# Two attention layers and two gated layers: norms of the gated layers on ScalarE, q's phi over ScalarE and VectorE, scans fetched from ScalarE, output units between q units

## Chip, cores, metric

One core of a Trainium2 chip. The metric is the device time of one execution in microseconds; before, the median of 3 runs is 1562.31 us (1561.06 to 1563.51). Engines go by the profile's names: PE (TensorE's matmuls), PEld (its weight loads), DVE (VectorE), ACT (ScalarE), POOL (GpSimd) and SP (SyncE, which issues DMAs).

## The reference, cut

S = 2048 rows (16 tiles of 128), D = 1024, F = 3584, 32 heads of 32. Four layers in turn, A B A B, with the same weights for both A and both B:

```python
def _A_ref(x, wqkv, wo):
    q, k, v = ...                      # x @ wqkv, by heads
    phi = lambda t: jnp.where(t > 0, t + 1, jnp.exp(t)) + 1e-6
    pq, pk = phi(q), phi(k)
    kv = jnp.einsum("bhsd,bhse->bhde", pk, v)
    z = jnp.einsum("bhsd->bhd", pk)
    num = jnp.einsum("bhqd,bhde->bhqe", pq, kv)
    den = jnp.einsum("bhqd,bhd->bhq", pq, z)[..., None] + 1e-6
    return (num / den) ... @ wo

def _B_ref(x, w_gate, w_up, w_down):
    h = (x @ w_gate) * (x @ w_up)
    return h @ w_down

x = x + _A_ref(_layernorm(x), A_wqkv, A_wo)
x = x + _B_ref(_layernorm(x), B_w_gate, B_w_up, B_w_down)
...                                    # the same two again
```

## The kernel before, in words

Nothing is scheduled by a compiler: the order in which the Python code emits instructions is the order on each engine, and every engine works strictly through its own row of instructions. An instruction that waits holds up all that stands behind it on its engine, DMA issues on SP too. x stays in SBUF (`X`, bf16). The eight large tiles `K[0]` to `K[7]`, and `W`, `TX`, `ST`, `MX`, are used again and again for different things; eight PSUM banks `Q[0]` to `Q[7]` are handed out in turn by `mm_tile`, so a matmul group can start when the group eight places before it has been read out of its bank.

**Layer A** (`layer_A`) runs in units, each a group of matmuls into one bank and what reads it out. k units (`k_unit`) give pk; 16 xk units give X^T pk (16 matmuls, a copy on ACT, L327); 32 q units (`q_unit`, two for a tile of rows) do 8 matmuls and `phi`: an exponential on ACT (L295), a minimum on DVE (L296) and, again from the bank, a maximum on DVE (L297). After a tile's second q unit `over_den` (L366) multiplies and sums on DVE, and SP transposes the tile by DMA (`tx`, L274). `kv_unit` and 16 kvo units (`kvo_unit`, one matmul each, copied by ACT at L394 into `KVo`) put kv and wo together. 32 output units (`out_unit`) do 8 matmuls each, and DVE adds the bank to X (`add_x`, L397).

In the first layer A, **scans** run beside this: gate, up and down weights are loaded in 42 pieces of 512 KB, and ACT squares and sums each (`scan_step`, L213) for a scale of each matrix (`scale_sum`, `scale_pow`, into `fac` and `kap`). Pieces share a few buffers, and a piece is fetched when its buffer's last piece has been scanned (`scan_fetch`, L198), by SP.

**The turn to a gated layer.** The last q units and the first output units alternate in a loop of nine (L672). Beside the output units the norm of the next layer is made for the first 8 tiles: `norm_fill` with DVE's statistics (L245, L249), POOL's power (L251 to L270) and ACT's application (`ln_apply_act`, L272) into `ST`, which holds four tiles, so the second four wait for the transposes of the first. `t_fill` (L466) forms sums of transposed tiles on DVE. `prep` converts a unit's weights on ACT (L435) and forms four sums (L438), here on POOL.

**Layer B** (`layer_B`) computes gate and up with a seven-product scheme on 2 x 2 blocks: for a unit u of 14, `gate_step(u, p)` does product p (8 matmuls into two banks) and reads it out. Product 1 needs only transposed tiles; 5, 6 and 4 need the first, second and fourth `t_fill` sum, 7 the third. The down weights get the same kind of sums in the first B layer (`down_prep`: fetch, scale on ACT, four sums on DVE, store to DRAM), spread over the units.

The order around the change, in the words of the code: `spread(main, fill)` emits a unit of main and then its share of fill. The two lines that set the turn are

```python
        spread(o[18:26], fill[9] + norm_fill(1, 1, xn_b, True))
        spread(o[26:], t_fill() + prep(1, nc.gpsimd) + (list(down_prep(0)) if first_A else []))
```

## Time and profile before

| | us |
|---|---|
| median of 3 runs | 1562.31 |
| the profiled execution | 1563.76 |
| its span | 1562.0 |
| PE busy | 1489.7 (95%) |
| DVE busy | 1114.4 (71%) |
| ACT busy | 691.9 (44%) |
| mean granted clock of TensorE | 0.986 |

Span is from the first instruction to the last; the execution's own time is a little longer. A row of the timeline gives start, duration, engine, line, operation, output and inputs, a count of merged instructions and, in brackets, the idle time before it and what ended it. A row of the groups gives busy time and mean ns of one, then the idle time before them.

### The profile page before, as it was taken

How to read it: one execution, taken by the hardware profiler on the slowest of the kernel's cores; microseconds unless marked ns; L12 is line 12 of the kernel's file. 1: busy time of each engine (PE TensorE's matmuls, PEld its weight loads, DVE VectorE, ACT ScalarE, POOL GpSimd, SP SyncE). 2: the span in 40 equal slices, each digit the busy share in tenths (PEclk: the TensorE clock that was granted, in tenths of full speed). 3: DMA queues.
4: the chain of work that ended last, by engine and by line, in shares of the span. 5: the costliest groups of instructions: out<-in, count | busy, mean ns of one | idle time of the engine just before them, and what ended most of it. 6: DMA issues, size and time to landing. Idle time of an engine off the chain costs nothing.

```text
span 1562.0 us, 18309 instructions
## 1 busy us (share of the span) xinstructions
PE 1489.7 (95%) x6893; PEld 678.7 (43%) x6995; DVE 1114.4 (71%) x1834; ACT 691.9 (44%) x834; POOL 121.8 (8%) x194
## 2 busy tenths in 40 slices
PE   9899798599999999999999998979999999999999
PEld 3344343244444444444444444434444444444444
DVE  7766697688878467776668778977777755777633
ACT  4976653478750066661013224136665004666300
POOL 3500022200001000000110000340000000000000
PEclk9999999799999999999999999989999999999999
DMA  7957725377656523324752014162233573332342
GB/s 223 201 176 207 226 59 112 112 213 220 192 182 210 134 81 89 101 76 167 200 145 67 15 29 114 27 115 82 81 82 101 171 227 101 95 94 81 128 173 84
DMA packets 277049, 202.79 MB, mean 130 GB/s; under 512 B 102112, under 2 KB 264160, under 8 KB 273376
## 3 DMA queue, kind: packets, MB, share of 16 engines
q1 hardware_dynamic: 276960, 201.62, 46.0%
q8 instruction: 54, 0.88, 0.2%
q14 instruction: 35, 0.29, 0.1%
HBM read 160.43 MB, written 17.04 MB: 114 GB/s over the span
## 4 chain that ended last, share of the span: by engine, by line
PE 84%; DVE 7%; DMA 3%; ACT 3%; issue 2%; SPq 1%; POOL 0%; ACTq 0%; DVEq 0%
PE Q L473 43%; PE Q L725 22%; PE Q L307 9%; PE Q L325 7%; PE Q L405 3%; DMA XT<-ST 1%; DVE X L397 1%; DVE W L296 1%; DVE TX L438 1%; DVE st L245 1%; SPq L133 1%; ACT K L213 1%; ACT W L295 1%; DVE MX L369 1%; DVE K L297 1%
## 5 line engine op out<-in xcount | busy, mean ns | idle before, releaser
L473 PEld LDWEIGHTS <-K 128*128 128x128 f16 x3136 | 307.7, 98 | 409.8 <-issue 39.6
L473 PE MATMUL Q<-XT,K 128*128 128x512 bf16 (+1 forms) x1732 | 398.8, 382 | 35.1 <-DVE X L397 28.6
L725 PE MATMUL Q<-K,K 128*128 128x512 f16 (+1 forms) x1596 | 340.8, 375 | 1.0 <-DVE X L732 1.0
L473 PE MATMUL Q<-TX,K 128*128 128x512 f16 x1344 | 308.5, 379 | 3.8 <-ACT MX L495 2.1
L435 ACT ACTIVATE K<-K,fac 128x2048 f16<-128x2048 bf16 x112 | 218.3, 2000 | 128.2 <-DMA K<-in_B_w_gate_dram 127.4
L725 PEld LDWEIGHTS <-K 128*128 128x128 f16 x1596 | 155.1, 98 | 185.1 <-issue 1.3
L438 DVE TENSOR_TENSOR K<-K 128x1024 f16<-128x1024 f16 (+1 forms) x228 | 146.9, 665 | 35.5 <-ACT K L435 33.5
L295 ACT ACTIVATE W<-Q 128x512 bf16<-128x512 f32 x128 | 76.2, 599 | 211.0 <-PE Q L307 198.1
L438 DVE TENSOR_TENSOR W<-MX,Q 128x512 f16<-128x512 f32 x176 | 116.6, 684 | 32.0 <-ACT MX L495 18.0
L307 PE MATMUL Q<-K,K 128*128 128x512 bf16 x498 | 117.5, 387 | 5.7 <-DVE W L296 4.9
L438 DVE TENSOR_TENSOR W<-W,Q 128x512 f16<-128x512 f32 x160 | 105.6, 684 | 18.1 <-ACT W L495 11.5
L307 PE MATMUL Q<-K,XT 128*128 128x512 bf16 x500 | 113.6, 379 | 2.0 <-DMA XT<-ST 0.8
L495 ACT COPY MX<-Q 128x512 f32<-128x512 f32 x120 | 69.3, 585 | 100.3 <-PE Q L473 100.3
L296 DVE TENSOR_SCALAR W<-W 128x512 bf16<-128x512 bf16 x128 | 46.7, 365 | 72.0 <-ACT W L295 72.0
L495 ACT COPY W<-Q 128x512 f32<-128x512 f32 x104 | 60.4, 585 | 76.8 <-PE Q L473 76.2
L438 DVE TENSOR_TENSOR K<-K,K 128x512 f16<-128x512 f16 (+1 forms) x148 | 87.7, 597 | 4.2
L438 DVE TENSOR_TENSOR K<-W,Q 128x512 f16<-128x512 f16 x56 | 38.4, 687 | 72.6 <-PE Q L473 72.6
L245 DVE BATCH_NORM_STATS2 st<-X 128x6 f32<-128x512 bf16 x128 | 80.9, 673 | 3.5 <-DMA X<-in_A_x_dram 3.5
L307 PEld LDWEIGHTS <-K 128*128 128x128 bf16 x512 | 50.6, 100 | 67.6 <-DMA K<-ST 5.4
L251 POOL TENSOR_SCALAR ve<-mv 128x1 f32<-128x1 f32 x64 | 15.5, 242 | 819.7 <-DVE mv L249 819.7
L732 DVE SCALAR_TENSOR_TENSOR W<-Q,kap,X 128x512 f32<-128x512 f32 x32 | 24.0, 750 | 77.6 <-PE Q L725 77.6
L307 PEld LDWEIGHTS <-XT 128*128 128x128 bf16 x512 | 49.6, 98 | 61.7 <-ACT XT L290 1.4
(90 smaller groups left out, 1294.0 us busy)
## 6 DMA issues: line engine op xcount, KB each, us to landing
K<-WD SPq DMA_DIRECT2D x28, 1792.0 KB, 7.4
K<-in_B_w_gate_dram SPq DMA_DIRECT2D x70, 512.0 KB, 4.2
K<-in_B_w_up_dram SPq DMA_DIRECT2D x67, 512.0 KB, 4.9
K<-in_A_wqkv_dram SPq DMA_DIRECT2D x10, 1024.0 KB, 7.8
K<-in_B_w_down_dram SPq DMA_DIRECT2D x19, 512.0 KB, 5.2
WD<-K SPq DMA_DIRECT2D x10, 512.0 KB, 2.9
X<-in_A_x_dram SPq DMA_DIRECT2D x16, 256.0 KB, 5.3
out_dram<-X SPq DMA_DIRECT2D x31, 128.0 KB, 1.7
```

The costliest lines, as they stand in the source:

```text
L245: nc.vector.bn_stats(out=stat[t][0][:, c, :], in_=X[:, t, c * NB:(c + 1) * NB])
L295: nc.scalar.activation(out=e, in_=ps, func=ACT.Exp)
L296: nc.vector.tensor_scalar(out=e, in0=e, scalar1=1.0, scalar2=1e-6, op0=ALU.min, op1=ALU.add)
L307: nc.tensor.matmul(out=ps, lhsT=xt[:, k, tl * P:(tl + 1) * P], rhs=w[:, k, :], start=(k == 0), stop=(k == KD - 1))
L325: nc.tensor.matmul(out=ps, lhsT=xn_a[t][:, j * P:(j + 1) * P], rhs=pk[t][:, n * NB:(n + 1) * NB], start=(t == 0), stop=(t == NT - 1))
L405: nc.tensor.matmul(out=ps, lhsT=xT[t // TPG][:, c, tl * P:(tl + 1) * P], rhs=KVo[n][:, c, :], start=(c == 0), stop=(c == KD - 1))
L435: nc.scalar.activation(out=b.bitcast(F16), in_=b, func=ACT.Copy, scale=fac[:, m:m + 1])
L438: eng.tensor_tensor(out=o, in0=a, in1=b, op=op)
L473: nc.tensor.matmul(out=pair[m], lhsT=stationary(n, p, m, k), rhs=moving[p][:, k, :], start=(p in (1, 2, 5) and k == 0), stop=(k == KH - 1) ...
L495: nc.scalar.copy(out=snaps[u, p][:, m, :], in_=a[m])
L725: nc.tensor.matmul(out=ps_[:, lo:hi], lhsT=act[:, u, j * P:(j + 1) * P], rhs=w[:, u, lo:hi], start=(p in (1, 2, 5) and u == 0), stop=(u == ...
L732: stt(out=o, in0=ps_, scalar=kap[:, 0:1], in1=x, op0=ALU.mult, op1=ALU.add)
```

## The change

- `ln_act` and `norm_act` are new: the norms of a gated layer's first 8 tiles, three ACT passes each (a sum for the mean, a square with a sum for the variance, the application), with POOL's small operations between them. The second four tiles go to buffers of their own (`xn_c`, in K[0] to K[3]).
- `phi` can be split: ACT writes x + 1 + 1e-6 to SBUF as a second pass over the bank, and DVE takes the maximum in SBUF. It is used for q tiles 13 to 15 of the first A layer and for all q tiles of the second.
- The scans: more of them in the four-piece buffers (`EARLY` 30, `MID` 39), three for each of the first six q tiles, fetched by ACT from piece 14 on.
- The kvo units stand one q unit later, five or six after each of q units 20 to 22.
- `prep(0)` has its sums on DVE; `prep(1)` and the scan-dependent `down_prep` move: units 0 and 1 of `down_prep` (scale on DVE) into the first A layer, `prep(1)` into the gated layer's unit 0, and later fetches one unit earlier.
- The norm's pieces stand between the output units from the fifth round of the loop on, and `t_fill` behind the last four output units.

In the built program the eight banks Q[0] to Q[7] are called Q_83 to Q_90, K[0] to K[7] are K_74 to K_81, and XT_69 and XT_70 hold the transposed tiles of the first and second four.

On ACT, at the first turn, the rows behind the last q unit stood like this (the exponential of q unit 31, eight applications, the conversion of unit 1, the first `down_prep`, then the copies of product 1):

```order
L295 ACTIVATE W<-Q_84 128x512
L272 ACTIVATE ST<-X,off,rstd 128x1024 x8
L435 ACTIVATE K_80<-K_80,fac 128x2048 x2
L532 ACTIVATE K_74<-K_74,fac 128x2048
L491 COPY MX<-Q_83 128x512
L491 COPY MX<-Q_84 128x512
```

and the last rows ahead of product 1's copies are now (L285 a pass with the sum for the mean, L289 with the sum of squares, L295 the application; eight like them stand between these and q unit 31):

```order
L285 ACTIVATE K_76,sm<-X 128x1024
L289 ACTIVATE K_75,ss<-X,nm 128x1024
L295 ACTIVATE K_74<-X,of,rs 128x1024
L285 ACTIVATE K_77,sm<-X 128x1024
L289 ACTIVATE K_76,ss<-X,nm 128x1024
L295 ACTIVATE K_75<-X,of,rs 128x1024
L289 ACTIVATE K_77,ss<-X,nm 128x1024
L295 ACTIVATE K_76<-X,of,rs 128x1024
L295 ACTIVATE K_77<-X,of,rs 128x1024
L519 COPY MX<-Q_83 128x512
L519 COPY MX<-Q_84 128x512
L463 ACTIVATE K_80<-K_80,fac 128x2048 x2
```

The conversion of unit 1 (K_80) moved from ahead of product 1's copies to behind them, and the applications now have their own sums ahead of them, on the same engine.

On DVE, in the same place, the last bank sums (X<-X,Q) and the four `t_fill` sums (the rows with XT) stood like this:

```order
L438 TENSOR_TENSOR TX<-XT_70,XT_69 128x2048
L397 TENSOR_TENSOR X<-X,Q_88 128x512
L438 TENSOR_TENSOR TX<-XT_70,TX 128x2048
L438 TENSOR_TENSOR XT_70<-XT_70 128x2048
L397 TENSOR_TENSOR X<-X,Q_89 128x512
L438 TENSOR_TENSOR TX<-XT_69,TX 128x2048
L397 TENSOR_TENSOR X<-X,Q_90 128x512
L397 TENSOR_TENSOR X<-X,Q_83 128x512
L397 TENSOR_TENSOR X<-X,Q_84 128x512
```

and now:

```order
L425 TENSOR_TENSOR X<-X,Q_88 128x512
L425 TENSOR_TENSOR X<-X,Q_89 128x512
L466 TENSOR_TENSOR TX<-XT_70,XT_69 128x2048
L425 TENSOR_TENSOR X<-X,Q_90 128x512
L466 TENSOR_TENSOR TX<-XT_70,TX 128x2048
L425 TENSOR_TENSOR X<-X,Q_83 128x512
L466 TENSOR_TENSOR XT_70<-XT_70 128x2048
L425 TENSOR_TENSOR X<-X,Q_84 128x512
L466 TENSOR_TENSOR TX<-XT_69,TX 128x2048
```

Two and three `t_fill` sums stand ahead of the sums that free Q_83 and Q_84, where all four did.

On ACT in the first kvo stretch, the scans (the rows with acc) and what stands between them, from q unit 17 on, were

```order
L295 ACTIVATE W<-Q_84 128x512
L213 ACTIVATE K_74,acc<-K_74 128x2048
L295 ACTIVATE W<-Q_85 128x512
L213 ACTIVATE W,acc<-W 128x2048
L295 ACTIVATE W<-Q_86 128x512
L394 CAST K_77<-Q_87 128x512
```

and are now (the DMA rows are fetches of later pieces):

```order
L326 ACTIVATE W<-Q_84 128x512
L326 ACTIVATE W<-Q_85 128x512
L217 ACTIVATE W,acc<-W 128x2048
L209 DMA W<-in_B_w_down_dram 128x2x1024
L209 DMA K_74<-in_B_w_down_dram 128x2x1024
L209 DMA K_78<-in_B_w_down_dram 128x2x1024
L326 ACTIVATE W<-Q_86 128x512
L326 ACTIVATE W<-Q_87 128x512
L422 CAST K_77<-Q_88 128x512
```

Three of the scans moved to the q tiles ahead of this stretch, and the fetches moved from SP's row into ACT's.

The diff, cut to its core:

```diff
+    pb = [W[:, 6 * D + i * NB:6 * D + (i + 1) * NB] for i in range(4)]
     scan_b = [W[:, 6 * D:8 * D], K[0][:, HEAD:HEAD + 2 * D]]
-    scan_c = scan_b + [K[i][:, HEAD:HEAD + 2 * D] for i in (1, 2)]
+    scan_c = scan_b + [K[i][:, HEAD:HEAD + 2 * D] for i in (4, 5)]
+    xn_c = {TPG + i: tail(i, 0) for i in range(4)}
...
-    EARLY, MID = 22, 34
+    EARLY, MID = 30, 39
...
-    scanned = [0, 0]
+    scanned = [0, 0, EARLY]
...
+    def scan_fetch():
+
+        while scanned[1] < scanned[2]:
             i = scanned[1]
             if any(scan_buf[j] is scan_buf[i] for j in range(scanned[0], i)):
                 return
             src, k = scan_src(i)
-            load(scan_buf[i].rearrange("p (k n) -> p k n", k=k), src)
+            (nc.sync if i < 14 else nc.scalar).dma_start(out=scan_buf[i].rearrange("p (k n) -> p k n", k=k), in_=src)
             scanned[1] += 1
 
...
             scanned[0] += 1
-            scan_fetch(EARLY if i < EARLY - 2 else MID if i < MID - 2 else NSCAN)
             if i == EARLY - 1:
                 load_qkv(wv, 2)
+            elif i == EARLY - 2:
+                scanned[2] = MID
+            scan_fetch()
...
+    def ln_act(t, xn):
+
+        sm, nm, ss, ve, rstd, off = (small.tile([P, 1], F32, tag=n_, name=n_) for n_ in ("sm", "nm", "ss", "va", "rs", "of"))
+
+        def mean():
+            nc.scalar.activation(out=xn, in_=X[:, t, :], func=ACT.Identity, accum_out=sm[:])
+            nc.gpsimd.tensor_scalar(out=nm[:], in0=sm[:], scalar1=-1.0 / D, scalar2=None, op0=ALU.mult)
+
+        def var():
+            nc.scalar.activation(out=xn, in_=X[:, t, :], func=ACT.Square, bias=nm[:], accum_out=ss[:])
+            nc.gpsimd.tensor_scalar(out=ve[:], in0=ss[:], scalar1=1.0 / D, scalar2=1e-5, op0=ALU.mult, op1=ALU.add)
+            nc.gpsimd.tensor_tensor(out=rstd[:], in0=ve[:], in1=mhalf[:, 0:1], op=ALU.pow)
+            nc.gpsimd.tensor_tensor(out=off[:], in0=nm[:], in1=rstd[:], op=ALU.mult)
+
+        def apply():
+            nc.scalar.activation(out=xn, in_=X[:, t, :], func=ACT.Identity, scale=rstd[:], bias=off[:])
+        return mean, var, apply
...
-    def phi(ps, dst):
+    def phi(ps, dst, split=False):
 
         e = turn("e", eb)
+        if split:
+            x1 = turn("x1", pb)
+            nc.scalar.activation(out=e, in_=ps, func=ACT.Exp)
+            nc.scalar.activation(out=x1, in_=ps, func=ACT.Identity, bias=one6[:])
+            nc.vector.tensor_scalar(out=e, in0=e, scalar1=1.0, scalar2=1e-6, op0=ALU.min, op1=ALU.add)
+            nc.vector.tensor_tensor(out=dst, in0=x1, in1=e, op=ALU.max)
+            return
...
-            proj(t, wq[n], pqs[t][:, n * NB:(n + 1) * NB])
+            phi(proj_mm(t, wq[n]), pqs[t][:, n * NB:(n + 1) * NB], split)
...
-            nc.scalar.activation(out=r.bitcast(F16), in_=r, func=ACT.Copy, scale=fac[:, 2:3])
+            if u > 1:
+                nc.scalar.activation(out=r.bitcast(F16), in_=r, func=ACT.Copy, scale=fac[:, 2:3])
+            else:
+                nc.vector.tensor_scalar(out=r.bitcast(F16), in0=r, scalar1=fac[:, 2:3], scalar2=None, op0=ALU.mult)
...
+    def norm_act(g, slot_, dst):
+
+        f = [ln_act(t, dst[t]) for t in range(g * TPG, (g + 1) * TPG)]
+        tr = [lambda t=t: tx(dst[t], t, slot_) for t in range(g * TPG, (g + 1) * TPG)]
+        out_ = []
+        for i in range(TPG + 2):
+            for j, k in ((i, 0), (i - 1, 1), (i - 2, 2)):
+                if 0 <= j < TPG:
+                    out_.append(f[j][k])
+                    if k == 2:
+                        out_.append(tr[j])
+        return out_
...
-        q = [q_unit(t, n) for t in range(NT) for n in range(2)]
+        q = [q_unit(t, n, li > 0 or t > 12) for t in range(NT) for n in range(2)]
...
-            scans()
+            scans(2 if t < 6 else 1)
         load_o()
         kv_unit()
         load_unit(0, 0)
         if first_A:
             scale_sum(0, 2)
+        for i in range(4):
+            q[16 + i]()
+            if i == 2:
+                scanned[2] = NSCAN
+                scans()
+        kvo = [lambda c=c: kvo_unit(c // 2, c % 2) for c in range(2 * KD)]
         for i in range(3):
-            q[16 + i]()
+            q[20 + i]()
+            do(kvo[16 * i // 3:16 * (i + 1) // 3])
             scans()
-        kvo = [lambda c=c: kvo_unit(c // 2, c % 2) for c in range(2 * KD)]
-        for i in range(4):
-            q[19 + i]()
-            do(kvo[4 * i:4 * i + 4])
             if i == 1 and first_A:
                 scale_pow(0, 2)
-            scans()
         o = [out_unit(t, n) for t in range(NT) for n in range(2)]
         o = [o[i] for i in (0, 2, 4, 1, 3, 5)] + o[6:]
-        norm = norm_fill(0, 0, xn_b, True)
-        fill = [[]] + [prep(0, nc.gpsimd)[i:i + 2] for i in (0, 2)] + [[]] * 3 + [norm[0:2], norm[2:4], norm[4:8], norm[8:]]
+        norm = norm_act(0, 0, xn_b) + norm_act(1, 1, xn_c)
+        fill = [[]] + [prep(0)[i:i + 2] for i in (0, 2)] + [[]]
         for i in range(9):
             q[23 + i]()
             do(o[2 * i:2 * i + 1])
-            do(fill[i])
+            if i < 4:
+                do(fill[i])
+            else:
+                do(norm[2 * i - 8:2 * i - 6])
             do(o[2 * i + 1:2 * i + 2])
-            if i < 3:
-                scans()
-            if i == 4 and first_A:
-                scale_sum(2, 3)
-            if i == 7 and first_A:
-                scale_pow(2, 3)
-        load_unit(1, 1)
+            if first_A:
+                if i == 3:
+                    scale_sum(2, 3)
+                elif i == 4:
+                    dp[0][0]()
+                elif i == 5:
+                    scale_pow(2, 3)
+                elif i == 6:
+                    dp[1][0]()
+        down = list(dp[0][1:]) + list(dp[1][1:]) if first_A else []
+        late = norm[10:]
+        for i in range(10):
+            o[18 + i]()
+            do(late[len(late) * i // 10:len(late) * (i + 1) // 10])
+            do(down[i:i + 1])
+            if i == 5:
+                load_unit(1, 1)
         load_unit(2, 2)
-        spread(o[18:26], fill[9] + norm_fill(1, 1, xn_b, True))
-        spread(o[26:], t_fill() + prep(1, nc.gpsimd) + (list(down_prep(0)) if first_A else []))
+        if first_A:
+            dp[2][0]()
+        spread(o[28:], t_fill())
...
-            dp = [down_prep(u) for u in range(NU)] if fetch else []
...
             for u in range(NU):
                 n = u + 1
-                pr = prep(base + n) if n < NU and (n > 1 or ps == 1) else [lambda: None] * 4
-                mine = [dp[i] for i in range(len(dp)) if i > 0 and max(0, i - 2) == u]
+                pr = prep(base + n) if n < NU else [lambda: None] * 4
+                mine = [dp[u + 2]] if fetch and u + 2 < NU else []
+                nxt = [dp[u + 3]] if fetch and u + 3 < NU else []
                 gate_step(u, 1)
-                for x in mine:
-                    x[0]()
                 gate_step(u - 1, 4)
                 do(pr[0:2])
-                for x in mine[1:]:
-                    x[1]()
                 gate_step(u, 2)
                 pr[2]()
                 gate_step(u - 1, 3)
                 gate_step(u, 6)
-                for x in mine[:1]:
+                for x in mine:
                     x[1]()
                 pr[3]()
                 gate_step(u, 5)
                 gate_step(u, 7)
                 for x in mine:
                     x[2]()
+                for x in nxt:
+                    x[0]()
```

11 lines of the change are left out of this document (5 added, 6 removed).

## The prediction

> **What bounds the kernel now.** I read the page's busy times first, then the windows view cut at the joints of the program (columns: stretch, its length, then busy time and instructions of PE, PEld, DVE, ACT, POOL, the granted clock, DMA share and GB/s), then the list of what PE waited for.
>
> ```profile
> PE 1489.7 (95%) x6893; PEld 678.7 (43%) x6995; DVE 1114.4 (71%) x1834; ACT 691.9 (44%) x834; POOL 121.8 (8%) x194
> ...
> 167.40:197.50 30.10, 20.64 (x83) 8.53 (x82) 17.64 (x31) 19.71 (x29) 0.71 (x1) 0.89 0.88 264
> ...
> 240.20:319.10 78.90, 52.24 (x230) 23.13 (x232) 53.31 (x91) 31.87 (x30) 19.94 (x29) 0.87 0.53 132
> 319.10:946.80 627.70, 625.54 (x2915) 286.49 (x2956) 459.18 (x782) 258.75 (x311) 20.65 (x48) 1.00 0.46 130
> 946.80:968.50 21.70, 17.70 (x83) 7.87 (x83) 18.38 (x28) 12.13 (x23) 0.00 (x0) 1.00 0.57 156
> ...
> 1010.10:1060.30 50.20, 40.29 (x174) 17.55 (x176) 39.06 (x55) 17.77 (x18) 19.35 (x25) 0.90 0.48 89
> ...
> PE Q L473 <- DVE X L397: 30.3, 3, 20.8
> PE Q L393 <- DVE W L297: 9.8, 6, 4.4
> ...
> 1009.91 27.79 PE L405 MATMUL Q<-K,K 128*128 128x512 bf16 x126
> ```
>
> TensorE is the bound: 625.54 of 627.70 us in the long stretch at full clock. The last row prices a matmul: 16 output units of 8 make 128 (two records are missing) in 27.79, so 0.216 us each. That gives each joint an ideal by its matmul count. First kvo stretch (q units 16 to 23 and 16 kvo units, 80 matmuls): 17.3, so 12.8 of 30.1 are lost. First turn to a gated layer (16 output units, then 13 products of 8: 232): 50.1, so 28.8 of 78.9 are lost. Second kvo stretch: 21.7 against 17.3, 4.4 lost. Second turn (16 output units, 6 products: 176): 38.0, 12.2 of 50.2 lost. Together 58.2 us are lost in four places, waits and half-speed restarts after them (clock 0.87 to 0.90). The change works on these four, so I price them one by one.
>
> **The two turns.** T is the end of q unit 31's matmuls (first turn: 238.34 + 1.89 = 240.2).
>
> ```profile
> 238.34 1.89 PE L307 MATMUL Q<-K,K 128*128 128x512 bf16 x8
> ...
> 248.10 4.63 ACT L272 ACTIVATE ST<-X,off,rstd 128x1024 bf16<-128x1024 bf16 x4 [7.24 <-POOL off L270]
> ...
> 268.26 3.53 ACT L272 ACTIVATE ST<-X,off,rstd 128x1024 bf16<-128x1024 bf16 x3 [2.62 <-DMA XT<-ST]
> 275.66 11.28 POOL L438 TENSOR_TENSOR K<-K 128x1024 f16<-128x1024 f16 x4 [10.59 <-ACT K L435]
> 275.85 3.00 DVE L438 TENSOR_TENSOR TX<-XT,XT 128x2048 f16<-128x2048 bf16 x1 [9.87 <-DMA XT<-ST]
> 289.27 0.59 PE L473 MATMUL Q<-XT,K 128*128 128x512 bf16 x1 [20.81 <-DVE X L397]
> 319.07 1.89 PE L473 MATMUL Q<-TX,K 128*128 128x512 f16 x8 [2.14 <-ACT MX L495]
> ...
> 1046.77 4.89 PE L473 MATMUL Q<-XT,K 128*128 128x512 bf16 x12 [7.79 <-DVE X L397]
> ...
> 1272.13 1.22 DVE L438 TENSOR_TENSOR TX<-XT,XT 128x2048 f16<-128x2048 bf16 x1
> ```
>
> Now the second group's norms end at 271.79, since their statistics stand late on DVE and they write the ST that the first group's transposes still read. Their transposes land 4.06 later, and the first `t_fill` starts at 275.85. The `t_fill` sums take 3.00 beside POOL's four `prep` sums, and PE waits for the bank sums (L397) queued among them. Without POOL's sums the same sum takes 1.22 (last row).
>
> The change takes the statistics off DVE, gives the second group its own buffers and takes `prep` off POOL. What is late next is ACT: behind q unit 31 stand there its exponential and identity, 10 passes with a sum (4 means, 6 squares) and 7 applications.
>
> ```profile
> L251 POOL TENSOR_SCALAR ve<-mv 128x1 f32<-128x1 f32 x64 | 15.5, 242 | 819.7 <-DVE mv L249 819.7
> ...
> L253 POOL TENSOR_TENSOR rstd<-ve,mhalf 128x1 f32<-128x1 f32 x64 | 37.5, 586 | 5.3
> ...
> L213 ACT ACTIVATION_READ_ACCUMULATOR K<-K 128x1 f32 x34 | 7.4, 219 | 0.0
> ...
> L263 DVE TENSOR_SCALAR ST<-X,mv,rstd 128x1024 bf16<-128x1024 bf16 x20 | 10.2, 533 | 0.2
> ...
> L270 POOL TENSOR_SCALAR off<-mv,rstd 128x1 f32<-128x1 f32 x27 | 7.9, 309 | 1.4
> ...
> L397 DVE TENSOR_TENSOR X<-X,Q 128x512 bf16<-128x512 bf16 x64 | 40.5, 673 | 0.0
> ...
> L435 ACT ACTIVATE K<-K,fac 128x2048 f16<-128x2048 bf16 x112 | 218.3, 2000 | 128.2 <-DMA K<-in_B_w_gate_dram 127.4 <-PE Q L725 0.8
> ...
> L438 DVE TENSOR_TENSOR K<-K 128x512 f16<-128x512 f16 x20 | 8.4, 418 | 0.0
> ```
>
> An application is 1.16 (4 in 4.63). A pass with a sum of this size is not in the trace: from below it is half of a 2048-wide scan's 1.89 (rows in the next part), so 0.95; from above one application plus the read of the accumulator, 1.16 + 0.22, so 1.4. I take 1.3. POOL's part for a tile, 0.242 + 0.586 + 0.309 = 1.14, has two ACT passes beside it, except for the last tile (0.3 uncovered). Sum: 1.1 + 10 x 1.3 + 7 x 1.16 + 0.3 = 22.5, and with 4.06 for the transposes the first `t_fill` starts at T + 26.6. DVE then runs sum, `t_fill`, sum, `t_fill` in turn: bank Q_83 is free at 26.6 + 2 x (1.22 + 0.67) = T + 30.4, Q_84 1.9 later. PE ends its output units at T + 27.8, so it waits 2.6, then 1.0 more between the two halves (1.9 less four matmuls). In the first unit ACT now converts the next unit between two bank copies (two L435 of 2.0, 4.0 in all), which in before stood ahead of PE's start: about 1.0 more before product 7. So 50.1 + 4.6 = 54.7 in place of 78.9: **24.2 saved**. DVE's added work behind T is two `down_prep` of 2.7 (twice a 1024-wide scale of 0.53, L263, and four 512-wide sums of 0.42, L438); with 16 bank sums of 0.67 that is 16.3 of 27.8 us, and the idle rest covers the one `over_den`. Without that cover banks would free late by what is over. Bounds: 27 saved with the 0.95 pass, 17 if the transposes wait on SP behind the WD stores and the loads of unit 1, which now stand between them.
>
> In the second turn the first product's banks belong to output units 26 and 27, whose sums stood behind a `t_fill` (7.79 waited) and now stand ahead of all. PE goes on at once; product 6 needs the second `t_fill` at T + 29.7 and is reached at T + 31.3. Only the 1.0 at product 7 is left: 38.0 + 1.0 for 50.2, **11.2 saved**, from 7 (`t_fill` 4 later) to 12.2.
>
> **The two kvo stretches and the scans.**
>
> ```profile
> 107.72 0.59 ACT L295 ACTIVATE W<-Q 128x512 bf16<-128x512 f32 x1
> 108.20 1.91 ACT L213 ACTIVATE K<-K 128x2048 bf16<-128x2048 bf16 x1
> 110.00 0.20 ACT L213 ACTIVATION_READ_ACCUMULATOR K<-K 128x1 f32 x1
> 110.09 0.59 ACT L295 ACTIVATE W<-Q 128x512 bf16<-128x512 f32 x1
> ...
> 134.80 0.52 SPq L133 DMA_DIRECT2D K<-in_B_w_up_dram  x1
> ...
> 171.97 2.97 SPq L133 DMA_DIRECT2D K<-in_B_w_up_dram  x1
> ...
> 183.15 1.91 ACT L213 ACTIVATE W<-W 128x2048 bf16<-128x2048 bf16 x1 [8.46 <-DMA W<-in_B_w_down_dram]
> ...
> 194.09 2.13 ACT L394 CAST K<-Q 128x512 bf16<-128x512 f32 x4
> ...
> W<-in_B_w_down_dram SPq DMA_DIRECT2D x5, 512.0 KB, 4.7
> ```
>
> On ACT a scan takes 1.89 (108.20 to 110.09), an exponential behind other work 0.48, a cast 0.52. In the first kvo stretch a scan waits 8.46 for a load that stood on SP behind wo and unit 0; the exponentials queued behind it hold PE's banks (4.4 in the list of waits). The change leaves 4 of 7 scans here, three of them ahead of what the output units need, and ACT fetches them itself. Count from the start of q unit 16: the first scan starts at 5.8 (three q units of 1.73 and an exponential). Then come 3 scans 5.7, 3 fetches, 4 exponentials 2.1 and 15 casts 7.9. A fetch on ACT is not in the trace: from SP's rows 0.5, or 2.97 where the queue is backed up, from below nothing. I take 0.5, as SP pays where its fetches stand apart: 23.0 in all. Its first load, out at 8.2 and landing in 4.7, is due at 13. I allow 1 for the 3 MB of other loads beside it: 24.0, so **6.1 saved**; 3 if the load takes 8, 7.6 with free fetches.
>
> Beside the output half of the scans (units t = 0 to 7) PE needs 38 matmuls each, 8.2 us. ACT gets three scans for two in six of them: 5.7 + 2 x 0.48 + 1.4 x 0.48 = 7.3, with three fetches at 0.5 it is 8.8. It falls 3.6 behind and makes that up in the last two (5.4 + 1.0 against 8.2). PE does not see it: eight banks, and 40.84 of 41.00 busy there now.
>
> ```profile
> 124.00:165.00 41.00, 40.84 (x204) 19.16 (x206) 30.23 (x45) 27.78 (x38) 0.00 (x0) 1.00 0.70 199
> ...
> 963.72 0.38 PE L393 MATMUL Q<-ST,W 128*128 128x512 bf16 x1 [2.56 <-DVE W L297]
> ...
> L295 ACT ACTIVATE W<-Q 128x512 bf16<-128x512 f32 x128 | 76.2, 599 | 211.0 <-PE Q L307 198.1 <-remote 6.8 <-DVE K L297 4.8
> ...
> L297 DVE SCALAR_TENSOR_TENSOR W<-Q,W 128x512 bf16<-128x512 f32 x64 | 44.3, 692 | 2.6
> ...
> L477 DVE TENSOR_TENSOR K<-W 128x512 f16<-128x512 f16 x168 | 71.4, 425 | 5.8
> ```
>
> By the Trainium skill, page "DMA: Bandwidth & Descriptors", section "Issuing engines are not separate DMA queues", a second issuing engine saves only the time to issue. By it the first kvo stretch would gain only what the order of the loads gives, some 3 instead of 6; the 8.46 stood on SP's order as well as on the transfer, so the trace leaves both open.
>
> In the second kvo stretch PE waited 2.56 for a bank that DVE frees (L297, behind an `over_den`). Split, DVE does a maximum in SBUF (L477: 0.425 for 0.692) and ACT frees the bank, for one more ACT pass, about L295's 0.6. ACT is then the bound there: 9.8 to the end of q unit 20's phi (five q units and 1.1), then 15 casts 7.9 and two phi 2.2: 19.9 for 21.7, **1.4 saved** with 0.4 for gaps; none to 3.
>
> **Sum.** 24.2 + 11.2 + 6.1 + 1.4 = 42.9. The profiled execution took 1563.76 (span 1562.0): 1520.9. The median of the runs, 1562.31, lies 1.45 lower, which gives 1519.4; I say 1520.
>
> **Rivals.**
> - *ACT is the new chain.* The passes cost 1.4 and POOL's 1.14 lies bare for each tile (4 x 1.14, and 1 for the passes), or SP holds the transposes. The `t_fill` sums start 6 to 7 later in both turns: 24 becomes 18, 11 becomes 7, and with 3 from the kvo stretch the sum is 29: 1533, to 1540. For it: ACT is strictly in order there. Against: 0.3 bare by the order of its rows.
> - *The fetches land no earlier*: 3 lost, 1522; inside the range. For it: the same 3 MB stand beside it; against: they are now issued ahead of the kv unit.
> - *Slower: fetches on ACT cost what backed-up ones cost SP.* With c for a fetch, ACT falls 6 x (7.3 + 3c - 8.2) + 2 x (5.4 + 2c - 8.2) = 22c - 11 behind, and the kv unit waits for its casts behind them. At 2.97 that is 54: 1573. It decides from c = 2.45. Against: SP's long rows stand behind four loads of 1 MB issued in a row; spaced ones take 0.5.
> - *No change*: no more than a fifth of the waits goes, because banks are held by something else in the same places: 1560 to 1565. Against: the rows name what holds them, and the change moves just that.
>
> **Chances.** Forecast (1511 to 1530) 0.58; fetches no earlier 0.10; ACT the new chain 0.17; between that and no change 0.04; no change 0.04; slower 0.07. A measurement tells some 0.2% from no change. The range, 1509 to 1540, takes in the first two rivals; above it stay 0.14 and below it a little.
>
> **What the profile would show.** Right: PE's wait for DVE's L397 sums at the first turn under 6 us, none at the second; `t_fill` sums at 1.2; the last norm at T + 22; the 8.46 wait gone; ACT's fetches near 0.5. Wrong: PE idle in the stretch of units t = 0 to 7, a kv unit waiting for ACT's casts, `t_fill` waiting for transposes past T + 30, or PE waiting for ACT's copies all through the first gated layer.

## The result, and the profile after

The changed kernel takes 1523.96 us (median of 4, 1522.62 to 1526.45) against 1562.36 in the same session: a ratio of 0.9756, 95% interval 0.9739 to 0.9773. The forecast was 1520. The profiled execution took 1522.62, its span is 1520.8: 41.2 us less than before's 1562.0, where the sum on record said 42.9.

The page's busy line after, and the windows view cut at the same joints (kv unit, first kvo stretch, first turn, second kvo stretch, second turn; T is again the end of q unit 31's matmuls):

```profile
PE 1490.2 (98%) x6995; PEld 677.9 (45%) x6995; DVE 1075.2 (71%) x1804; ACT 744.6 (49%) x934; POOL 87.3 (6%) x195
...
163.36:169.41 6.05, 3.89 (x65) 3.65 (x64) 5.66 (x10) 5.49 (x7) 0.00 (x0) 1.00 0.66 180
169.41:195.88 26.47, 19.62 (x84) 8.27 (x82) 23.77 (x41) 17.98 (x32) 0.71 (x1) 0.94 0.81 225
237.50:293.74 56.24, 51.74 (x233) 22.95 (x231) 38.61 (x65) 38.13 (x48) 8.96 (x22) 0.97 0.68 173
921.69:939.41 17.72, 17.58 (x83) 7.83 (x81) 13.79 (x24) 13.59 (x27) 0.00 (x0) 1.00 0.68 187
981.29:1019.11 37.82, 37.82 (x176) 17.11 (x175) 25.50 (x37) 27.94 (x38) 7.83 (x22) 1.00 0.50 112
```

PE is busy for the same 1490 us, now 98% of the span. The second turn has no idle time left (37.82 busy of 37.82), and the second kvo stretch hardly any (17.58 of 17.72). What remains is named by the head of the list of PE's waits:

```profile
PE Q L338 <- DMA K<-ST: 4.8, 1, 4.8
PE Q L353 <- DVE K L328: 4.7, 2, 3.3
PE Q L501 <- DVE X L425: 4.0, 1, 4.0
PE Q L421 <- DMA TX<-in_A_wo_dram: 3.2, 1, 3.2
PE Q L413 <- ACT K L355: 2.2, 2, 1.9
PE Q L338 <- DVE part L233: 2.1, 1, 2.1
PE Q L421 <- DMA ST<-in_A_wo_dram: 1.3, 1, 1.3
```

The 20.8 at the first turn is a 4.0 (product 1 for the bank sums), the 7.79 at the second is gone, and so is the 4.4 in the first kvo stretch. The waits for wo stayed (3.2 and 1.3; before, 2.65 and 0.59). The two longest rows are not of the change: the 4.8 stands at 44 us in the first layer, where before waited 4.9, and the 4.7 was 4.6. Two rows are new: the kv unit waits for ACT's xk copies (L413 <- L355), and a matmul of the first kvo stretch waits 2.1 for a bank that `scale_pow` reads on DVE (L233).

The kernels of the study, in us: stretches and span from the windows view of one profiled execution each, the median over all executions. In kernels whose edit leaves a stretch alone, the first turn lies within 0.7 of the changed kernel's, the second turn and the second kvo stretch within 0.2, but the kv unit scatters from 6.0 to 8.6 and the first kvo stretch from 25.8 to 28.1 where nothing there was touched. The ratio is to before, run beside it; its interval reaches 0.0014 to 0.0020 to each side, 2 to 3 us. Before itself took 1562.4 beside the changed kernel and 1565.0 to 1565.7 beside the others, so a ratio of theirs can't be set against 0.9756 to better than some 0.002: a2_no_split loses 6.5 in its stretch, 5.9 by the medians and 3.5 by the ratios. Parts are therefore compared by their stretches, and sums by the medians.

| kernel | kv unit | kvo 1 | turn 1 | kvo 2 | turn 2 | span | median | ratio |
|---|---|---|---|---|---|---|---|---|
| before | 3.6 | 30.1 | 78.9 | 21.7 | 50.2 | 1562.0 | 1562.4 | 1 |
| changed | 6.1 | 26.5 | 56.2 | 17.7 | 37.8 | 1520.8 | 1524.0 | 0.9756 |
| turn_sp_clear | 8.6 | 26.4 | 52.2 | 17.5 | 38.0 | 1521.0 | 1520.3 | 0.9714 |
| turn_stats_dve | 6.1 | 28.1 | 64.0 | 17.5 | 38.7 | 1530.8 | 1532.0 | 0.9789 |
| turn_one_buffer | 6.1 | 27.2 | 57.3 | 17.5 | 38.0 | 1521.7 | 1523.7 | 0.9739 |
| turn_prep_pool | 6.3 | 27.9 | 60.6 | 17.5 | 38.7 | 1526.2 | 1527.2 | 0.9756 |
| turn_three_old | 6.1 | 27.7 | 67.5 | 17.7 | 43.0 | 1540.2 | 1539.9 | 0.9841 |
| t_fill_old_place | 7.3 | 25.8 | 59.4 | 17.7 | 37.8 | 1526.8 | 1526.5 | 0.9756 |
| a2_no_split | 6.1 | 26.5 | 56.2 | 24.2 | 37.8 | 1528.1 | 1529.8 | 0.9778 |
| scan_fetch_sp | 6.8 | 30.4 | 56.9 | 17.7 | 37.8 | 1527.0 | 1528.8 | 0.9769 |
| wo_act | 6.1 | 25.5 | 56.2 | 17.7 | 37.8 | 1521.1 | 1522.0 | 0.9726 |
| two_scans_late | 3.6 | 25.2 | 55.9 | 17.7 | 37.8 | 1517.9 | 1520.8 | 0.9719 |
| four_edits | 3.6 | 27.3 | 52.3 | 17.7 | 37.8 | 1515.0 | 1515.7 | 0.9686 |
| four_edits_split | 3.6 | 18.1 | 51.0 | 17.7 | 37.8 | 1505.3 | 1506.9 | 0.9629 |

### The profile page after: what moved, and what is told of

Same layout as the page of the kernel before. It is cut to its first block, busy times and chain, and to the rows that moved or that the text cites. A ratio compares the mean times of both kernels' runs of the same rounds, so it can differ in the third digit from the quotient of the medians.

```text
span 1520.8 us, 18444 instructions
## 1 busy us (share of the span) xinstructions
PE 1490.2 (98%) x6995; PEld 677.9 (45%) x6995; DVE 1075.2 (71%) x1804; ACT 744.6 (49%) x934; POOL 87.3 (6%) x195
## 4 chain that ended last, share of the span: by engine, by line
PE 86%; ACT 6%; DVE 3%; DMA 3%; issue 1%; SPq 1%; POOL 0%; ACTq 0%; DVEq 0%
PE Q L501 45%; PE Q L786 22%; PE Q L338 8%; PE Q L433 5%; PE Q L353 5%; ACT K L217 2%; ACT W L326 1%; DVE W L327 1%; DVE K L328 1%; DMA TX<-in_A_wo_dram 1%; DMA K<-in_B_w_up_dram 1%; DMA X<-in_A_x_dram 1%; ACT K L422 0%; DMA K<-in_B_w_gate_dram 0%; DMA W<-in_B_w_down_dram 0%
## 5 line engine op out<-in xcount | busy, mean ns | idle before, releaser
L501 PE MATMUL Q<-XT,K 128*128 128x512 bf16 (+1 forms) x1792 | 407.2, 380 | 4.0 <-DVE X L425 4.0
L466 DVE TENSOR_TENSOR K<-K 128x1024 f16<-128x1024 f16 (+1 forms) x244 | 157.2, 666 | 37.2 <-ACT K L463 35.3
L466 DVE TENSOR_TENSOR W<-MX,Q 128x512 f16<-128x512 f32 x176 | 116.5, 684 | 30.4 <-ACT MX L523 18.0
L326 ACT ACTIVATE W<-Q 128x512 bf16<-128x512 f32 x90 | 53.0, 596 | 140.2 <-PE Q L338 124.6
L466 DVE TENSOR_TENSOR W<-W,Q 128x512 f16<-128x512 f32 x160 | 105.6, 683 | 11.4 <-ACT W L523 4.9
L466 DVE TENSOR_TENSOR K<-K,K 128x512 f16<-128x512 f16 (+1 forms) x148 | 87.6, 597 | 4.2
L466 DVE TENSOR_TENSOR K<-W,Q 128x512 f16<-128x512 f16 x56 | 38.4, 686 | 72.9 <-PE Q L501 72.8
L505 DVE TENSOR_TENSOR K<-W 128x512 f16<-128x512 f16 x168 | 71.3, 425 | 5.8
L217 ACT ACTIVATE K<-K 128x2048 bf16<-128x2048 bf16 x36 | 69.0, 1918 | 6.8 <-DMA K<-in_B_w_down_dram 3.2
L327 DVE TENSOR_SCALAR W<-W 128x512 bf16<-128x512 bf16 x90 | 33.3, 370 | 47.2 <-ACT W L326 47.1
```

The lines of the kernel that those rows point to most:

```text
L217: nc.scalar.activation(out=scan_buf[i], in_=scan_buf[i], func=ACT.Square, accum_out=acc[:, m, c:c + 1])
L326: nc.scalar.activation(out=e, in_=ps, func=ACT.Exp)
L327: nc.vector.tensor_scalar(out=e, in0=e, scalar1=1.0, scalar2=1e-6, op0=ALU.min, op1=ALU.add)
L466: eng.tensor_tensor(out=o, in0=a, in1=b, op=op)
L501: nc.tensor.matmul(out=pair[m], lhsT=stationary(n, p, m, k), rhs=moving[p][:, k, :], start=(p in (1, 2, 5) and k == 0), stop=(k == KH - 1) ...
L505: nc.vector.tensor_tensor(out=hA[i][:, u, :], in0=gu[:, 0, :], in1=gu[:, 1, :], op=ALU.mult)
```

## Experiments at the turns

**The statistics (turn_stats_dve).**

```diff
-        norm = norm_act(0, 0, xn_b) + norm_act(1, 1, xn_c)
+        norm = norm_fill(0, 0, xn_b, True) + norm_fill(1, 1, xn_c, True)
```

> The changed kernel with one part undone, in both turns: the statistics of the 8 tiles made by DVE again (two half rows of 0.64 us and an aggregation of 0.21 for a tile), ACT only applies; the second group's own buffers, POOL's absence from prep and the order of t_fill stay. Theory P (what the prediction says of the first part: the statistics had to leave DVE, because they stand late there): the last norm later than T + 22 by 3 us or more, time 1527 or more. Rival D (DVE has room for 6 us of statistics between T and T + 20, and ACT loses 16 of its 24 passes; what counted was the buffer, the prep and the order): last norm between T + 19 and T + 23, time 1521 to 1525.

The last application on ACT and the first `t_fill` sum on DVE (L278 the application, L466 the sum), by the timeline of this kernel, whose T is 238.7:

```profile
263.82 4.63 ACT L278 ACTIVATE K<-X,off,rstd 128x1024 bf16<-128x1024 bf16 x4 [22.41 <-POOL off L276]
...
260.94 1.28 DVE L251 BATCH_NORM_STATS2 st<-X 128x6 f32<-128x512 bf16 x2
...
273.21 1.22 DVE L466 TENSOR_TENSOR TX<-XT,XT 128x2048 f16<-128x2048 bf16 x1 [7.21 <-DMA XT<-K]
```

ACT stands idle for 22.4 us; the last statistics end at T + 23.5, later than the changed kernel's last norm. The norms end at T + 29.7; 7.7 us are lost in the first turn (63.95 against 56.24), 0.9 in the second. Theory P holds: on DVE the statistics stand behind `over_den`, bank sums and the `down_prep` sums, and ACT can do nothing until they are made.

**The second group's buffer, POOL's sums, the order (turn_one_buffer, turn_prep_pool, t_fill_old_place).**

```diff
-        ... + norm_act(1, 1, xn_c)
+        ... + norm_act(1, 1, xn_b)            # turn_one_buffer
...
+        do(prep(1, nc.gpsimd))                # turn_prep_pool, and no prep(1) in unit 0
         spread(o[28:], t_fill())
...
-        spread(o[28:], t_fill())              # t_fill_old_place
+        spread(o[26:], t_fill() + [lambda: None] * (7 if first_A else 4))
```

> The changed kernel with one part undone, in both turns: the second group's norms go to ST again, which the first group's transposes read, instead of to K[0] to K[3]. Theory B (the shared buffer was a main cause, as the prediction says of before): ACT's first pass over tile 5 waits for a transpose that lands at about 248.9 instead of starting at 246.5, tile 7's for one that lands near 252.7, so the norms end 2 to 3 us later, each turn loses 2 to 3, 1528 to 1530. Rival (the shared buffer only hurt because the statistics were late): nothing, 1524.

> The changed kernel with one part undone, in both turns: unit 1 is converted by ACT behind the last norm and its four sums made by POOL, beside the t_fill sums, and unit 0 of the gated layer no longer does this work. Theory V (POOL's sums slow DVE's t_fill sums, the mechanism that the prediction takes from 3.00 against 1.22 us): the t_fill sums take 2.5 to 3 us, PE's wait at the first turn grows from 4.0 to about 7.5 and a wait of 2 to 4 comes at the second, from which 1 us comes back since ACT has no conversion in unit 0: 1527 to 1530. Rival (the t_fill sums were slow because the DMA of that time ran beside them): they stay at 1.22 and the time goes down by about 1, 1523.

> The changed kernel with one part undone: in both turns the t_fill sums stand among the bank sums where the kernel before had them (the first behind output unit 26's sum), all else stays. In the first turn the two banks of product 1 are then read behind all four t_fill sums. Theory E (the order adds to the early norms in the first turn and is only a second cover in the second): PE waits about 7.4 instead of 4.0 in the first turn, nothing in the second, where the transposes have landed 25.2 after the last q unit, so a sum behind one t_fill ends at 27.1, ahead of PE at 27.6: 1527. Rival O (the order is the cause of the second turn's gain): 5 to 8 us lost in the second turn too, 1533 or more.

One row of ACT in turn_one_buffer; the `t_fill` sums on DVE and the four sums on POOL in turn_prep_pool; PE's wait in t_fill_old_place:

```profile
247.64 1.06 ACT L285 ACTIVATE ST<-X 128x1024 bf16<-128x1024 bf16 x1 [1.74 <-DMA XT<-ST]
```

```profile
265.62 2.20 DVE L466 TENSOR_TENSOR TX<-XT,XT 128x2048 f16<-128x2048 bf16 x1 [4.68 <-DMA XT<-K]
...
268.34 2.54 DVE L466 TENSOR_TENSOR TX<-XT,TX 128x2048 f16<-128x2048 bf16 x1
...
264.62 11.29 POOL L466 TENSOR_TENSOR K<-K 128x1024 f16<-128x1024 f16 x4 [6.72 <-ACT K L463]
```

```profile
PE Q L501 <- DVE X L425: 7.4, 1, 7.4
```

The shared buffer costs one wait of 1.74 and 1.0 us of the first turn (57.27), not 2 to 3, which is hardly more than that stretch varies by; the median is the changed kernel's. So the rival's figure came: with the norms early, the transposes have mostly landed. POOL's sums double the `t_fill` sums, from 1.22 to between 2.20 and 2.54, and cost 4.4 in the first turn (60.60): theory V. In the second they cost 0.9, where it named a wait of 2 to 4. The DMA of that time is the same in both kernels (2.00 MB from 263 to 276 us, 1.96 in the changed one), so it isn't the cause. The old order costs the 7.4 that was worked out, 3.2 in the first turn (59.44) and nothing in the second: theory E.

**Three parts together (turn_three_old).** The edits of turn_stats_dve, turn_one_buffer and turn_prep_pool in one kernel.

> The changed kernel with three parts of the turn undone together: statistics on DVE, the second group in ST again, unit 1's sums on POOL beside the t_fill sums. The new order (t_fill behind the last four output units, so that in the second turn the bank sums of output units 26 and 27 stand ahead of all four) stays. Theory O (in the second turn the order alone removes the 7.79 wait, as the prediction says): there PE goes from output unit 31 to product 1 without a wait (27.6 us from the last q unit to product 1, as in the changed kernel), and only the later products wait, 3 to 6 us; the first turn loses 12 to 16 of its 23 us; 1540 to 1546. Rival P (the parts that make the norms early removed it): product 1 waits 5 us or more in the second turn, and the time goes above 1546.

PE's rows at the first and at the second turn:

```profile
277.89 1.86 PE L501 MATMUL Q<-XT,K 128*128 128x512 bf16 x4 [12.94 <-DVE X L425]
...
1022.94 3.62 PE L501 MATMUL Q<-XT,K 128*128 128x512 bf16 x16
1030.00 5.16 PE L501 MATMUL Q<-TX,K 128*128 128x512 f16 x16 [3.44 <-DVE TX L466]
```

At the second turn product 1 starts without a wait although the norms are late again; only the product that needs a `t_fill` sum waits. So theory O holds there: the order alone removes the 7.79. With t_fill_old_place, which loses nothing there, it follows that the second turn has two covers, the order and the early norms, either of which is enough for product 1. The first turn loses 11.3 of its 22.7 (67.49), a little under the 12 to 16 of theory O, and the single losses of the three parts (7.7, 1.0, 4.4) come to 13.1, so they overlap.

Of the other 11.4, two rows of the kernel before name 5.0, ahead of a product in its first gated unit (the prediction shows the second such wait, 2.14 at 319.07):

```profile
298.70 2.00 ACT L532 ACTIVATE ST<-ST,fac 128x2048 f16<-128x2048 bf16 x1 [5.24 <-DMA ST<-in_B_w_down_dram]
...
301.23 3.61 PE L473 MATMUL Q<-XT,K 128*128 128x512 f16 x16 [2.88 <-ACT MX L495]
```

PE waited there for ACT's copies, and ACT stood behind scales of `down_prep` that waited 5.24 and 4.17 for their loads. In turn_three_old, where `down_prep` keeps its new place, PE has no such wait in that unit. The prediction took this gain in through the ideal of the stretch and did not name it. The rest is a shorter wait at product 1 (12.94 and 1.20 for 20.81); the order, which loses 3.2 when undone alone, belongs to it, and it was not taken apart further.

**SP's row (turn_sp_clear).**

```diff
+            held.append(store) if u < 2 else store()     # the WD stores of units 0 and 1
...
-            if i == 5:
-                load_unit(1, 1)
+        load_unit(1, 1)                                  # behind the last transpose
         load_unit(2, 2)
+            do(held)
```

> The changed kernel, with the four WD stores of the first two down units and the loads of unit 1 issued by SP behind the last transpose of the first turn instead of between the transposes. Theory Q (SP's row: the stores and loads between the transposes hold them up; in the first turn the first t_fill sum starts 6.6 us after the last norm, in the second, where nothing stands between, 3.8): the first t_fill starts at T + 25.2 instead of T + 28.0, PE's wait for the bank sums falls from 4.0 to about 1.2, 2.8 us less, 1521. Rival R (four transposes in a row take that long by themselves, whatever else SP issues): t_fill stays at T + 28, 1524.

The last transposes on SP in the changed kernel, then its first `t_fill` sum and PE's first products; behind them the first `t_fill` sum of this kernel (T is 240.5):

```profile
251.30 1.31 SPq L135 DMA_DIRECT2D WD<-K  x2
252.71 3.00 SPq L301 DMA_TRANSPOSE XT<-K  x1
255.76 0.70 SPq L135 DMA_DIRECT2D K<-in_B_w_gate_dram  x1
256.51 0.83 SPq L135 DMA_DIRECT2D K<-in_B_w_up_dram  x1
257.44 5.86 SPq L301 DMA_TRANSPOSE XT<-K  x3
...
265.52 1.23 DVE L466 TENSOR_TENSOR TX<-XT,XT 128x2048 f16<-128x2048 bf16 x1 [4.84 <-DMA XT<-K]
...
269.13 5.11 PE L501 MATMUL Q<-XT,K 128*128 128x512 bf16 x16 [4.00 <-DVE X L425]
274.08 3.62 PE L501 MATMUL Q<-TX,K 128*128 128x512 f16 x16
```

```profile
265.43 1.23 DVE L466 TENSOR_TENSOR TX<-XT,XT 128x2048 f16<-128x2048 bf16 x1 [1.70 <-DMA XT<-K]
```

The first `t_fill` comes at T + 24.9 instead of T + 28.0; PE's wait falls from 4.0 to 1.6 in two pieces. Theory Q holds, and the gain is 4.0 (56.2 to 52.2) instead of 2.8. The rest is the clock: after the 4.0 wait, 16 matmuls took 5.11 where the next 16 took 3.62, and the turn's granted clock was 0.97; with two short waits it is 1.00. The kv unit happened to take 8.6 in the profiled execution, which hides the gain in the span; the median is 3.7 lower.

How the stores and loads held the transposes is not parted by this run. They stood ahead of them on SP, and they also slowed them: in the changed kernel each of the last four transposes held SP for 1.27 to 3.00 and landed 4.7 after its issue (median), here 1.23 to 1.29 and 3.2. Nor are stores and loads parted. The expectation says that nothing stands between in the second turn, but unit 1's loads do (SP issues them at 997.1 and 997.7, ahead of the last three transposes), and the first `t_fill` still starts 3.8 after the last norm. So the WD stores, which only the first turn has, probably weigh more.

## Experiments at the kvo stretches

**The split of phi (a2_no_split).**

```diff
-        q = [q_unit(t, n, li > 0 or t > 12) for t in range(NT) for n in range(2)]
+        q = [q_unit(t, n, li == 0 and t > 12) for t in range(NT) for n in range(2)]
```

> The changed kernel with one part undone: no split of phi in the second layer A (three tiles of the first keep it). The new place of the kvo units stays. Theory S (the split gave the second kvo stretch its gain, since DVE no longer reads the bank): that stretch goes from 17.7 back to 20 to 21.7 us and PE waits for DVE's maximum again, 1526 to 1528. Rival O (the kvo units one q unit later, five or six in a row, gave it): 17.5 to 18.5 us, no change in the total beyond 1 us.

PE in the second kvo stretch of this kernel:

```profile
935.20 0.38 PE L421 MATMUL Q<-TX,W 128*128 128x512 bf16 x1
939.70 0.38 PE L421 MATMUL Q<-ST,W 128*128 128x512 bf16 x1 [4.13 <-DVE W L328]
```

The stretch takes 24.2: theory S, and more than before's 21.7. With five or six kvo units in a row PE comes back sooner to a bank that DVE's maximum still has to read behind an `over_den` (the maximum at 938.96 follows the end of `over_den` at 938.7). So the new place of the kvo units, by the difference to before, costs 2.5 without the split; together they bring 4.0.

**Who fetches the scans (scan_fetch_sp).**

```diff
-            (nc.sync if i < 14 else nc.scalar).dma_start(out=scan_buf[i]...
+            nc.sync.dma_start(out=scan_buf[i]...
```

> The changed kernel with one part undone: all scan pieces fetched by SP; their number for each q tile and their buffers stay. Theory I (the engine counts, because on SP a fetch stands behind transposes that wait for over_den, 4 us of DVE work a tile): scans wait for their loads by several us more, the kv unit (6.1 us, 3.6 without a wait) and the first kvo stretch (26.5) take 5 to 12 us more together, 1530 to 1536. Rival, the rule weighed in the prediction (a second issuing engine saves only the time to issue): nothing is lost, and ACT, which pays 0.45 us for each of its fetches, gets some 11 us back, so the kv unit loses its wait: 1521 to 1524.

ACT's waits for scan loads from 95 to 205 us in this kernel and the longest waits in SP's own row there (95 to 200), then in the changed kernel a fetch on ACT with the instruction behind it:

```profile
ACT W L217 <- DMA W<-in_B_w_down_dram: 13.8, 5, 6.9
...
ACT K L217 <- DMA K<-in_B_w_down_dram: 4.2, 1, 4.2
```

```profile
SPq L301 <- DVE W L403: 57.9, 12, 8.8
```

```profile
103.51 0.38 ACTq L209 DMA_DIRECT2D K<-in_B_w_up_dram  x1
103.93 0.60 ACT L326 ACTIVATE W<-Q 128x512 bf16<-128x512 f32 x1 [0.45 <-ACT K L217]
```

From SP the scans wait 18.0 for their loads (3.7 in the changed kernel), and the kv unit and the stretch take 4.7 longer together (37.25 against 32.52), a little under the 5 that theory I gave as its least. Kernels with no edit there take 32.5 to 35.0, so 2.3 of it are clear of what these stretches vary by; the median is 4.9 higher. The rival fails: ACT saves 0.45 a fetch and spends more than that waiting. By the Trainium skill, page "DMA: Bandwidth & Descriptors", section "Issuing engines are not separate DMA queues", initiating from several engines only saves the initiating sequencer's time. The transfer is indeed no faster: pieces of the down weights land 4.2 and 5.2 after their issue from SP (median, into W and into K) and 4.4 and 5.2 from ACT.

What differs is the row in which the fetch stands. SP works through it in order, and its transposes wait for the last instruction of `over_den` on DVE (L403). Two of the six scan waits, 4.2 and 3.5, are for pieces that SP issued right behind such a transpose, 4.5 and 7.2 after their buffer had been scanned. The longest, 6.9, is another case: its piece was issued right behind two 1 MB loads of q, k and v weights (wqkv) and could be scanned 9.2 later. So the transposes explain part of the 18.0, not all of it.

**Two scans later (two_scans_late).**

```diff
-            scans(2 if t < 6 else 1)
+            scans(2 if t < 5 else 1 if t < 7 else 0)
...
+                if i < 2:
+                    scans()                  # behind q units 23 and 24
```

> The changed kernel with one edit: two of the scans beside q tiles 5 and 7 move behind q units 23 and 24. Theory L (the prediction's step that failed: ACT does not make up what it falls behind beside q tiles 0 to 7, since two of its scans wait 3.7 us for their loads, so the last xk copies come late and PE waits for them in the kv unit): ACT is 4 us earlier there, the kv unit goes from 6.1 to 3.6 us, 1521.5. Rival (the loads bind, so the same waits come back one scan later): kv unit still 5 or more, or the kvo stretch longer by what the kv unit gains: 1524.

ACT and PE around the kv unit of the changed kernel, then the kv unit's window in this one:

```profile
153.78 1.91 ACT L217 ACTIVATE K<-K 128x2048 bf16<-128x2048 bf16 x1 [3.18 <-DMA K<-in_B_w_down_dram]
...
157.42 1.91 ACT L217 ACTIVATE W<-W 128x2048 bf16<-128x2048 bf16 x1 [0.54 <-DMA W<-in_B_w_down_dram]
...
166.90 1.07 ACT L355 CAST K<-Q 128x512 bf16<-128x512 f32 x2
...
167.53 0.22 PE L413 MATMUL Q<-K,K 128*128 128x128 bf16 x1 [1.89 <-ACT K L355]
```

```profile
162.72:166.30 3.58, 3.58 (x66) 3.57 (x65) 3.33 (x5) 1.29 (x3) 0.00 (x0) 1.00 0.69 192
```

The kv unit is at 3.6, as before the change, and the next stretch isn't longer (25.2): theory L. Both later kernels with this edit show 3.6 too; no other variant of the changed kernel is under 6.0. The edit takes the work of two scans away together with their waits, so alone it does not show that the loads are the cause. turn_sp_clear, which edits nothing there, supports it: its scan at this place waits 5.88 for its load instead of 3.18 and 0.54, and its kv unit takes 8.6. In both kernels the late piece is the one that ACT fetches 0.4 after SP has begun to issue the two 1 MB loads of wqkv; no run moved those. Nothing was given back behind q units 23 and 24 either: the first turn is at 55.9.

**wo earlier (wo_act), then four edits, then the split in the first layer.**

```diff
-            load(wo[n], wo_v[:, :, n * NB:(n + 1) * NB])
+            nc.scalar.dma_start(out=wo[n], in_=wo_v[:, :, n * NB:(n + 1) * NB])
...
+            if t == XT_ - 1:
+                load_o()                     # ahead of q tile 7's last scan
```

> The changed kernel with one edit: wo fetched by ACT, in the eighth q tile behind the last xk copy, ahead of that tile's last scan. In the changed kernel SP issues it at 173.8, behind the transpose of q tile 7, and PE waits 1.3 and 3.2 us for its halves in the first kvo stretch. Theory Q (the order on SP holds it; ST and TX are free since the last xk matmul at about 163): issued 5 to 9 us earlier, landing before 179, both waits gone, and with the half-speed restart behind them 5 us less in that stretch, 1519. Rival B (the loads beside it bind: at 360 GB/s whatever comes first, a scan piece or unit 0 is then late): less than 2 us in the sum of the kv unit and the kvo stretch, 1523 or more.

> The changed kernel with four edits that leave all work as it is: the stores and loads behind the first turn's transposes, wo fetched by ACT in q tile 7, two scans behind q units 23 and 24, and scale_pow for gate and up behind q unit 18, so that its bank is read ahead of an over_den. Theory A (what the single edits gave in their own stretches adds up: 4.0 in the turn, 2.5 in the kv unit, 1.3 to 3 in the first kvo stretch): 8 to 9 us less than the changed kernel, a ratio to before near 0.970, where the changed kernel had 0.9756. Rival B (the loads bind, and a wait removed in one place comes back in the next): 5 us or less.

> The same four edits, and the first kvo stretch made like the second: phi split from q tile 8 on (x + 1 + 1e-6 goes to the tails of K[6], since the scans use the first place), and its four scans and the two late ones all go behind q units 23 to 25, two each, with unit 0's conversion behind q unit 26. Theory D (with wo there in time, what is left of the first kvo stretch is DVE's over_den, which holds the banks that phi reads, as the run without the split shows in the second layer A): the stretch falls from 25 to about 18 us, a ratio to before near 0.966. Rival C (ACT, with six scans in 15.5 us of output units, falls behind and the norms start late): the stretch falls, but the time from the last q unit to product 1 grows by 3 us or more, ratio 0.968 or more.

PE in wo_act; PE's longest wait in four_edits; the first kvo stretch in four_edits_split:

```profile
180.87 1.89 PE L338 MATMUL Q<-K,K 128*128 128x512 bf16 x8 [1.84 <-DVE W L328]
182.59 0.38 PE L421 MATMUL Q<-TX,W 128*128 128x512 bf16 x1
187.09 0.58 PE L421 MATMUL Q<-ST,W 128*128 128x512 bf16 x1 [4.12 <-DVE W L328]
```

```profile
PE Q L421 <- DVE W L328: 6.6, 2, 4.9
```

```profile
166.88:184.93 18.05, 17.45 (x84) 7.86 (x82) 15.98 (x34) 13.90 (x27) 0.71 (x1) 1.00 1.10 299
```

With wo in time both waits for it are gone, and in their place PE waits 1.8 and 4.1 for DVE's maximum, in the pattern that a2_no_split shows in the second layer. The stretch gains 1.0, less than its scatter. Rival B's figure came (less than 2), but not by its cause, since wo and the scans no longer wait for loads there; and the order on SP, theory Q, was not all that held the stretch.

By the medians four edits bring 8.2, theory A's 8 to 9. The spans of the two profiled executions differ by only 5.8: the changed kernel's is the shortest of its four executions, this one's the second longest of five. In the traces the 4.0 in the turn and the 2.5 in the kv unit add up, while the stretch, at 27.3, keeps none of what wo and the earlier `scale_pow` should give; DVE's maximum takes it all. It is late by DVE's own row, which runs without a wait from 178.9 to 190.5, while the exponentials of ACT are there at 181.1. At 1515.74 us, ratio 0.9686 (0.967 to 0.9701), this is the fastest version here that computes what the reference does.

With phi split and the scans moved out of the stretch it takes 18.05, theory D, and the norms don't start late: the first turn is at 51.0 and its ideal is 50.1. How much of the 9.3 is the split and how much the scans' new place stays open. The ratio is 0.9629 (0.9615 to 0.9644). In this kernel the second layer A does not compute the reference. By the code, its split starts at the first q tile, and x + 1 + 1e-6 lands on norm tiles in K[6] that later xk units still read. In the first layer the split starts behind the xk units, so its stretch can be read as it stands, and the second layer's stretches are as long as elsewhere. A version with another place in the second layer was not run.

## Why the prediction was right, and which of its terms were off

| term, us saved | on record | measured |
|---|---|---|
| first turn | 24.2 | 22.7 |
| second turn | 11.2 | 12.4 |
| first kvo stretch | 6.1 | 3.6 |
| second kvo stretch | 1.4 | 4.0 |
| kv unit | 0 | -2.5 |
| q units 23 to 31 | 0 | 1.1 |
| sum | 42.9 | 41.2 |

The last row but one is 42.7 (197.5 to 240.2) against 41.6 (195.9 to 237.5); what is left ahead of the kv unit and in the gated layers comes to -0.1. The total is closer than its terms, since errors of both signs met: 6.5 too much in the first turn, the first kvo stretch and the kv unit, 4.9 too little in the other three. That part of the hit is luck. The two turns, 35.1 of the 41.2, came in the main by the mechanisms on record.

Two places of ACT's row in the changed kernel, a mean pass, a square pass and the last two applications at the first turn, and the last casts of the second kvo stretch:

```profile
248.62 1.04 ACT L285 ACTIVATE K<-X 128x1024 bf16<-128x1024 bf16 x1
...
249.66 1.13 ACT L289 ACTIVATE K<-X,nm 128x1024 bf16<-128x1024 bf16 x1
...
256.36 2.55 ACT L295 ACTIVATE K<-X,of,rs 128x1024 bf16<-128x1024 bf16 x2
...
938.46 3.18 ACT L422 CAST K<-Q 128x512 bf16<-128x512 f32 x6
```

- **First turn: mechanism right.** The 17 passes stand on ACT as counted; the last norm ends at T + 21.4 (T + 22 on record): the passes took 1.04 and 1.13 instead of 1.3, POOL's operations lay bare once for 1.03 instead of 0.3, and `t_fill` sums run at 1.22. The term that is short is the transposes: 6.6 from the last norm instead of 4.06. That SP's row might hold them was on record as a bound, and turn_sp_clear shows it. With 4.0 of wait came a slow restart (16 matmuls in 5.11 for 3.62) that the sum did not hold.
- **Second turn: right.** Product 1 goes on at once, and the 1.0 allowed at product 7 does not come.
- **Second kvo stretch: mis-sized.** ACT's row is as long as summed: its last cast ends at 941.64, 19.95 after the stretch begins, for 19.9. But PE goes on to the first output unit at 939.41, ahead of that cast; the prediction took the end of ACT's row for the end of PE's stretch, and the output unit needs the last column block only with its last matmul.
- **Kv unit: the step that failed.** The prediction let ACT fall 3.6 behind beside q tiles 0 to 7 and make it up in the last two, with nothing to spare (its 22c - 11 is 0 at c = 0.5), and put the scans' waits for loads at nothing. A fetch cost what it said (0.45 for 0.5), but two scans waited 3.7 for their loads, so the last xk copies came late and PE lost 2.5 in the kv unit. It was named as a sign of error, with the fetch as the cause; the rows point to the loads.
- **First kvo stretch: the waits changed owners.** The 8.46 is gone, and no scan waits for its load in this stretch, but wo still came late behind the transpose of q tile 7, and a bank of `scale_pow` stood behind an `over_den` (2.1). Behind those stands DVE's maximum, which the sum never priced in the first layer.
- Of the rivals, the slow one (fetches at 2.97 each) is out by the 0.45. (The prediction set the 2.97 behind four loads of 1 MB; it is itself the last of four in a row, two of 1 MB and two of 0.5.) The first (ACT the new chain) fits in one piece only, SP's hold on the transposes. The second (the fetches land no earlier) has its figure, about 3 lost in the first kvo stretch, but not its cause, since the scans' waits there are gone.
